# Attention rebuilt around pairs of heads, rows scattered into one region per expert, and slots read at a dynamic offset

## The chip, the core and the metric

One core of a Trainium2 chip. Five engines work side by side, each through its own instruction queue: PE (matmul; its weight loads are shown as PEld), DVE (vector), ACT (scalar), POOL and SP. SP issues most transfers; POOL issues those that cast or that scatter and gather by index. The metric is the device time of one launch in microseconds (us). The kernel before takes 1003.38 us (median of 3 runs, 1003.16 to 1006.25).

## The reference

Linear attention over 8 batch elements (B), 8 heads (H), 576 positions (S) and 64 dimensions (D), then a mixture of 8 experts of which each row uses one.

```python
def phi(x, c, s):                       # c, s: cosine and sine of the position
    r = np.maximum(x, 0.0)
    return np.concatenate([r * c, r * s], axis=-1)
q_p, k_p = phi(q, cos_w, sin_w), phi(k, cos_w, sin_w)
kv  = np.einsum('bhsf,bhsd->bhfd', k_p, v)
num = np.einsum('bhsf,bhfd->bhsd', q_p, kv)
den = np.einsum('bhsf,bhf->bhs', q_p, np.sum(k_p, axis=2))[..., None] + 1e-06
x   = (num / den)                       # to [B*S, H*D] = [4608, 512]
logits = x @ w_gate
e_idx  = np.argmax(logits, axis=1)
gate_w = softmax(logits)[np.arange(N), e_idx]
eom    = 1.0 / (1.0 + np.exp(-(x @ w_output_gate)))
for e in range(8):                      # w1: [512, 1024], w2: [1024, 512]
    mask = e_idx == e
    out[mask] = gate_w[mask, None] * eom[mask, e, None] * (np.maximum(x[mask] @ w1[e], 0) @ w2[e])
```

## The kernel before

**Start.** POOL issues the 16 loads of the expert weights (w1t, w2t, lines 121 and 122; f32 in memory, f16 on the core, so POOL's queue q0 casts them). SP's queue q1 takes everything else in.

**Attention**, for each batch element b. The 576 positions go in five chunks c of 128 (the last of 64), one position per partition. For each chunk SP loads qt, kt, vt for all heads (lines 147 to 151; a run of 64 numbers, 256 bytes, is one packet). ACT writes the cosine and sine halves of qp, DVE those of kp. PE multiplies kp by vt per head into kvp (line 171; the 65th column of vt is 1, which gives the sum of k_p), and DVE adds kvp to kvzg. PE transposes qp per head (tp, line 178), and ACT and DVE in turn copy that to qpt. Behind the five chunks PE transposes kvzg per head (tpk) and multiplies it by both gate matrices (kvgp), so that 16 columns of gate terms stand beside the 65. A second pass over the chunks multiplies qpt by the 81 columns per head (fx, line 204); DVE divides, sums the gate terms over the heads (glog), takes maximum, one-hot (oh_tab) and coefficient (coef_tab), and SP stores the row block xch as f16 to x_dram.

All f32 operations of PE are recorded twice per matmul, once per transpose.

**Routing** starts when all 40 chunks are done. Counts per chunk and expert give each expert's start among 42 slots of 128 rows. Then, chunk by chunk, PE ranks the rows, DVE forms dst_i, and POOL scatters the pair (row number, coefficient) to the table bucket (line 348). The table is read back (bidx) and gives the row indices for gather and scatter.

**Experts.** For each of 42 slots: PE reads the slot's expert into a register; POOL gathers 128 rows of x_dram into xg (line 371); PE transposes xg (xtsp), DVE copies that to xts; PE multiplies by w1t (hp, line 395), ACT rectifies into hs; in the next round of the loop PE transposes hs (htsp), DVE copies that to hts, PE multiplies by w2t (yp, line 406), DVE scales into ysb (line 410), and POOL scatters ysb to the output (line 411).

The order on each engine is made by a scheduler from the written program; an engine executes its rows in that order.

Of the kernel before, what the change touches and what calls it, by code (L numbers as in the profile page):

```python
# [10 lines left out]
F32 = mybir.dt.float32  # L12
F16 = mybir.dt.float16
I32 = mybir.dt.int32
ALU = mybir.AluOpType
# [5 lines left out]
def kernel(  # L21
# [24 lines left out]
    NCH = 5  # L46
    ROWS = [128, 128, 128, 128, 64]
    NG = B * NCH
    NSLOT = 42
    CAP = NSLOT * P  # L50
# [3 lines left out]
    tabs = ctx.enter_context(tc.tile_pool(name="tabs", bufs=1))  # L54
    dram = ctx.enter_context(tc.tile_pool(name="drampool", bufs=1, space=bass.MemoryType.DRAM))

    x_dram = dram.tile([N, DM], F16, name="x_dram")
    bucket = dram.tile([CAP, 2], F32, name="bucket")

# [3 lines left out]
    make_identity(nc, ident16[:])  # L63
    u128 = constp.tile([P, P], F32, name="u128")
    make_upper_triangular(nc, u128[:], val=1.0, diag=False)
    ones128 = constp.tile([P, P], F32, name="ones128")
    GP.memset(ones128[:], 1.0)

    s_i = constp.tile([P, NCH], I32, name="s_i")
    GP.iota(s_i[:], pattern=[[128, NCH]], base=0, channel_multiplier=1)  # L70
    th = constp.tile([P, NCH], F32, name="th")
# [3 lines left out]
    th2 = constp.tile([P, NCH], F32, name="th2")  # L75
# [5 lines left out]
    cosc = constp.tile([P, NCH], F32, name="cosc")  # L81
    sinc = constp.tile([P, NCH], F32, name="sinc")

    def поly(dst, coeffs, extra_mul, nm):
        acc = constp.tile([P, NCH], F32, name=nm)
        DVE.memset(acc[:], 0.0)
        for cc in reversed(coeffs):
            DVE.tensor_mul(acc[:], acc[:], th2[:])
            DVE.tensor_scalar_add(acc[:], acc[:], float(cc))
        DVE.tensor_mul(acc[:], acc[:], th2[:])  # L90
        DVE.tensor_scalar_add(acc[:], acc[:], 1.0)
        if extra_mul is not None:
            DVE.tensor_mul(dst[:], acc[:], extra_mul[:])
        else:
            DVE.tensor_copy(dst[:], acc[:])

    поly(sinc, sin_c, th, "acc_s")
    поly(cosc, cos_c, None, "acc_c")

    wg2 = constp.tile([P, H, 16], F32, name="wg2")  # L100
    SP.dma_start(wg2[0:64, :, 0:8], moe_w_gate.rearrange("(h p) e -> p h e", p=64))
    SP.dma_start(wg2[0:64, :, 8:16],
                 moe_w_output_gate.rearrange("(h p) e -> p h e", p=64))

    iota8 = constp.tile([P, E], F32, name="iota8")
    _i8 = constp.tile([P, E], I32, name="_i8")
    GP.iota(_i8[:], pattern=[[1, E]], base=0, channel_multiplier=0)
    DVE.tensor_copy(iota8[:], _i8[:])
    iota_slot = constp.tile([P, 1], F32, name="iota_slot")
    _is = constp.tile([P, 1], I32, name="_is")  # L110
    GP.iota(_is[:], pattern=[[1, 1]], base=0, channel_multiplier=128)
    DVE.tensor_copy(iota_slot[:], _is[:])
    mvals = constp.tile([P, NSLOT], F32, name="mvals")
    _im = constp.tile([P, NSLOT], I32, name="_im")
    GP.iota(_im[:], pattern=[[128, NSLOT]], base=0, channel_multiplier=0)
    DVE.tensor_copy(mvals[:], _im[:])
# [3 lines left out]
    for e in range(E):  # L120
# [3 lines left out]
    coef_tab = tabs.tile([P, NG], F32, name="coef_tab")  # L124
    oh_tab = tabs.tile([P, NG, E], F32, name="oh_tab")
    bidx = tabs.tile([P, NSLOT, 2], F32, name="bidx")
    gidx_i = tabs.tile([P, NSLOT], I32, name="gidx_i")
    sidx_i = tabs.tile([P, NSLOT], I32, name="sidx_i")
    slote_i = tabs.tile([P, 1], I32, name="slote_i")

    with tc.tile_pool(name="attn_b", bufs=2) as ap, \
         tc.tile_pool(name="attn_c", bufs=2) as ap2, \
         tc.tile_pool(name="pskv", bufs=3, space=bass.MemoryType.PSUM) as pskv, \
         tc.tile_pool(name="psgen", bufs=5, space=bass.MemoryType.PSUM) as psgen:

        for b in range(B):
            qpt = ap.tile([P, H, 576], F32, name=f"qpt{b}", tag="qpt")
            kvzg = ap.tile([P, H, 81], F32, name=f"kvzg{b}", tag="kvzg", bufs=1)
            GP.memset(kvzg[:], 0.0)

            for c in range(NCH):
                rows = ROWS[c]
                s0 = c * 128
                qt = ap2.tile([P, H, D], F32, name=f"qt{b}_{c}", tag="qt")
                kt = ap2.tile([P, H, D], F32, name=f"kt{b}_{c}", tag="kt")
                vt = ap2.tile([P, H, 65], F32, name=f"vt{b}_{c}", tag="vt")
                SP.dma_start(qt[0:rows, :, :],
                             q[b, :, s0:s0 + rows, :].rearrange("h s d -> s h d"))
                SP.dma_start(kt[0:rows, :, :],
                             k[b, :, s0:s0 + rows, :].rearrange("h s d -> s h d"))  # L150
                SP.dma_start(vt[0:rows, :, 0:64],
                             v[b, :, s0:s0 + rows, :].rearrange("h s d -> s h d"))
                GP.memset(vt[:, :, 64:65], 1.0)  # L153

                qp = ap2.tile([P, H, P], F32, name=f"qp{b}_{c}", tag="qp")
                kp = ap2.tile([P, H, P], F32, name=f"kp{b}_{c}", tag="kp")
                ACT.activation(qp[0:rows, :, 0:64], qt[0:rows, :, :], AF.Relu,
                               scale=cosc[0:rows, c:c + 1])
                ACT.activation(qp[0:rows, :, 64:128], qt[0:rows, :, :], AF.Relu,
                               scale=sinc[0:rows, c:c + 1])  # L160
                DVE.tensor_scalar(kp[0:rows, :, 0:64], kt[0:rows, :, :], 0.0,
                                  cosc[0:rows, c:c + 1], ALU.max, ALU.mult)
                DVE.tensor_scalar(kp[0:rows, :, 64:128], kt[0:rows, :, :], 0.0,
                                  sinc[0:rows, c:c + 1], ALU.max, ALU.mult)

                for hg in range(2):
                    kvp = pskv.tile([P, 4, 65], F32, name=f"kvp{b}_{c}_{hg}",
                                    tag="kvps")
                    for hh in range(4):
                        h = hg * 4 + hh  # L170
                        PE.matmul(kvp[:, hh, :], kp[0:rows, h, :],  # L171
                                  vt[0:rows, h, :], start=True, stop=True)
                    DVE.tensor_tensor(kvzg[:, hg * 4:(hg + 1) * 4, 0:65],  # L173
                                      kvzg[:, hg * 4:(hg + 1) * 4, 0:65], kvp[:],
                                      ALU.add)
                for h in range(H):
                    tp = psgen.tile([P, P], F32, name=f"tp{b}_{c}_{h}", tag="ps")
                    PE.transpose(tp[:, 0:rows], qp[0:rows, h, :],  # L178
                                 ident[0:rows, 0:rows])
                    if h % 2 == 0:  # L180
                        ACT.copy(qpt[:, h, s0:s0 + rows], tp[:, 0:rows])  # L181
                    else:
                        DVE.tensor_copy(qpt[:, h, s0:s0 + rows], tp[:, 0:rows])  # L183

            for h in range(H):
                tpk = psgen.tile([P, P], F32, name=f"tpk{b}_{h}", tag="ps")
                PE.transpose(tpk[0:64, :], kvzg[:, h, 0:64], ident[:, :])  # L187
                kvt_sb = tabs.tile([P, P], F32, name=f"kvt{b}_{h}", tag="kvt")
                ACT.copy(kvt_sb[0:64, :], tpk[0:64, :])  # L189
                kvgp = psgen.tile([P, 16], F32, name=f"kvgp{b}_{h}", tag="ps")  # L190
                PE.matmul(kvgp[:, :], kvt_sb[0:64, :], wg2[0:64, h, :],  # L191
                          start=True, stop=True)
                DVE.tensor_copy(kvzg[:, h, 65:81], kvgp[:, :])

            for c in range(NCH):
                rows = ROWS[c]
                s0 = c * 128
                g = b * NCH + c
                n0 = b * S + s0

                fx = [psgen.tile([P, 4, 81], F32, name=f"fx{g}_{i}", tag="ps")
                      for i in range(2)]
                for h in range(H):
                    PE.matmul(fx[h // 4][0:rows, h % 4, :],  # L204
                              qpt[:, h, s0:s0 + rows], kvzg[:, h, 0:81],
                              start=True, stop=True)
# [240 lines left out]
```

## Time and profile before

| | us |
|---|---|
| median of the runs | 1003.38 |
| profiled execution, span of the core | 1002.1 |
| first packets to first dense matmuls (kvp) | 0 to 121.6 |
| attention, one batch element | 62.26 |
| scatters to the table bucket | 610.8 to 792.9 |
| first hp matmul to the end of the last yp | 804.05 to 990.8 |

Share of the span that each engine is busy: PE 66%, DVE 38%, ACT 18%, POOL 15%. A row of the profile names line, engine, operation and the tiles (out<-in); PE's records overlap, so the time per matmul is read from start to start. Behind a row stands how long the engine was idle before it, and what ended that.

### The profile page before, as it was taken

What the parts mean: (1) busy time and instruction counts of PE and PEld (TensorE: products, weight loads), DVE (VectorE), ACT (ScalarE), POOL (GpSimd) and SP (SyncE); (2) the same over time, 40 slices, a digit from 0 to 9 for tenths busy, and PEclk for the clock granted to TensorE, in tenths of its full rate; (3) what the DMA queues carried; (4) which work ended last, traced back from release to release, by engine and by line L of the source; (5) the groups of instructions that cost most, each with busy time, mean ns of one, the idle gap of its engine ahead of it and who ended that gap; (6) DMA issues with size and microseconds to landing.
All of it is one profiled execution on the core that took longest, in us unless ns stands there. A gap on an engine that the chain in (4) does not pass through costs nothing.

```text
span 1002.1 us, 11193 instructions
## 1 busy us (share of the span) xinstructions
PE 662.7 (66%) x3257; PEld 496.6 (50%) x3257; DVE 377.0 (38%) x2049; ACT 177.9 (18%) x509; POOL 152.0 (15%) x245
## 2 busy tenths in 40 slices
PE   0113187997979979799797884223221099999994
PEld 0013176785867858578575683222211045555552
DVE  3101028456283562835528364111111033443342
ACT  1111001314123141231412210000000022222221
POOL 4110000000000000000000001222222134444441
PEclk9999999999999999999999999999999999999998
DMA  9999931412414124141241000000000112222220
GB/s 173 200 200 200 78 79 34 101 42 61 85 50 95 43 61 85 51 95 43 61 84 51 11 17 9 0 0 2 0 0 1 6 63 91 84 83 88 86 85 21
DMA packets 148858, 65.64 MB, mean 65 GB/s; under 512 B 128254, under 2 KB 141054, under 8 KB 148800
## 3 DMA queue, kind: packets, MB, share of 16 engines
q1 hardware_dynamic: 129600, 33.16, 17.5%
q0 software_dynamic: 19200, 31.77, 13.8%
q8 instruction: 29, 0.48, 0.2%
q14 instruction: 29, 0.24, 0.1%
HBM read 67.45 MB, written 15.81 MB: 83 GB/s over the span
## 4 chain that ended last, share of the span: by engine, by line
PE 50%; DMA 26%; DVE 13%; ACT 5%; issue 4%; SPq 1%; POOLq 0%; POOL 0%; ACTq 0%; DVEq 0%
DMA bucket<-pack,dst_i 14%; PE kvp L171 13%; PE fx L204 9%; PE hp L395 7%; DMA qt<-in_q_dram 7%; PE yp L406 7%; PE tp L178 5%; PE kvgp L191 4%; DVE xch L250 4%; DVE glog L215 2%; PE tpk L187 2%; DMA kt<-in_k_dram 2%; PE htsp L384 2%; DMA vt<-in_v_dram 2%; ACT kvt L189 1%
## 5 line engine op out<-in xcount | busy, mean ns | idle before, releaser
L178 PE MATMUL tp<-ident,qp 128*128 128x128 f32 (+1 forms) x320 | 101.2, 423 | 113.9 <-ACT qpt L181 36.9
L171 PE MATMUL kvp<-vt,kp 128*128 128x65 f32 (+1 forms) x640 | 145.6, 412 | 30.5 <-DMA vt<-in_v_dram 28.1
L171 PEld LDWEIGHTS kvp<-vt,kp 128*128 128x128 f32 (+1 forms) x640 | 143.3, 332 | 32.9 <-issue 32.0
L204 PE MATMUL fx<-kvzg,qpt 128*128 128x81 f32 (+1 forms) x640 | 136.1, 406 | 7.4 <-DVE glog L215 7.4
L204 PEld LDWEIGHTS fx<-kvzg,qpt 128*128 128x128 f32 (+1 forms) x640 | 128.9, 310 | 12.2 <-PE fx L204 10.6
L178 PEld LDWEIGHTS tp<-ident,qp 128*128 128x128 f32 (+1 forms) x320 | 55.4, 206 | 158.2 <-ACT qpt L181 74.1
L399 ACT ACTIVATE hs<-hp 128x512 f16<-128x512 f32 x84 | 50.2, 597 | 331.5 <-PE hp L395 331.5
L250 DVE TENSOR_SCALAR xch<-fx,rc 128x64 f16<-128x64 f32 (+1 forms) x320 | 86.8, 273 | 0.0
L395 PE MATMUL hp<-w1t,xts 128*128 x336 | 81.2, 385 | 7.5 <-DVE xts L390 7.5
L406 PE MATMUL yp<-w2t,hts 128*128 x336 | 79.4, 379 | 1.1 <-DVE hts L387 1.1
L173 DVE TENSOR_TENSOR kvzg<-kvzg,kvp 128x260 f32<-128x260 f32 x80 | 32.9, 418 | 110.5 <-PE kvp L171 110.5
L410 DVE TENSOR_SCALAR ysb<-yp,bidx 128x512 f32<-128x512 f32 x42 | 31.5, 751 | 112.8 <-PE yp L406 112.8
L215 DVE SCALAR_TENSOR_TENSOR glog<-fx,rc,glog 128x16 f32<-128x16 f32 (+1 forms) x280 | 62.9, 225 | 0.3
L181 ACT COPY qpt<-tp 128x128 f32<-128x128 f32 (+1 forms) x160 | 39.8, 252 | 119.5 <-PE tp L178 119.5
L183 DVE COPY qpt<-tp 128x128 f32<-128x128 f32 (+1 forms) x160 | 38.6, 266 | 47.8 <-PE tp L178 45.3
L341 DVE CAST dst_i<-dst_f 128x1 int32<-128x1 f32 (+1 forms) x40 | 6.1, 152 | 131.8 <-DMA bucket<-pack,dst_i 131.8
L406 PEld LDWEIGHTS <-hts 128*128 128x128 f16 x336 | 32.8, 98 | 40.6 <-DVE hts L387 1.2
L153 POOL MEMSET vt<- 128x8 f32 x40 | 4.4, 113 | 314.2 <-PE kvp L171 263.2
L395 PEld LDWEIGHTS <-xts 128*128 128x128 f16 x336 | 32.1, 98 | 39.7 <-DVE xts L390 9.1
L411 POOL DMA_INDIRECT out_dram<-ysb,sidx_i x42 | 42.6, 1014 | 56.1 <-DVE ysb L410 37.2
L348 POOL DMA_INDIRECT bucket<-pack,dst_i x40 | 38.6, 966 | 79.3 <-DVE dst_f L338 55.6
L371 POOL DMA_INDIRECT xg<-x_dram,gidx_i x42 | 40.8, 972 | 62.6 <-PE xtsp L377 45.9
(234 smaller groups left out, 661.1 us busy)
## 6 DMA issues: line engine op xcount, KB each, us to landing
qt<-in_q_dram SPq DMA_DIRECT2D x32, 256.0 KB, 3.9
w1t<-in_moe_w_dram POOLq DMA_DIRECT2D x8, 1024.0 KB, 46.4
kt<-in_k_dram SPq DMA_DIRECT2D x32, 256.0 KB, 3.5
vt<-in_v_dram SPq DMA_DIRECT2D x32, 256.0 KB, 3.2
w2t<-in_moe_w_dram POOLq DMA_DIRECT2D x8, 1024.0 KB, 44.0
x_dram<-xch SPq DMA_DIRECT2D x32, 128.0 KB, 1.7
qt<-in_q_dram SPq DMA_DIRECT2D x8, 128.0 KB, 2.8
kt<-in_k_dram SPq DMA_DIRECT2D x8, 128.0 KB, 3.4
```

What stands on the lines that cost most here:

```text
L171: PE.matmul(kvp[:, hh, :], kp[0:rows, h, :], vt[0:rows, h, :], start=True, stop=True)
L178: PE.transpose(tp[:, 0:rows], qp[0:rows, h, :], ident[0:rows, 0:rows])
L181: ACT.copy(qpt[:, h, s0:s0 + rows], tp[:, 0:rows])
L191: PE.matmul(kvgp[:, :], kvt_sb[0:64, :], wg2[0:64, h, :], start=True, stop=True)
L204: PE.matmul(fx[h // 4][0:rows, h % 4, :], qpt[:, h, s0:s0 + rows], kvzg[:, h, 0:81], start=True, stop=True)
L215: DVE.scalar_tensor_tensor(glog[0:rows, :], fx[h // 4][0:rows, h % 4, 65:81], rc[0:rows, h:h + 1], glog[0:rows, :], ALU.mult, ALU.add)
L250: DVE.tensor_scalar(xch[0:rows, h * 64:(h + 1) * 64], fx[h // 4][0:rows, h % 4, 0:64], rc[0:rows, h:h + 1], None, ALU.mult)
L371: GP.indirect_dma_start(out=xg[:], out_offset=None, in_=x_dram[:, :], in_offset=bass.IndirectOffsetOnAxis(ap=gidx_i[:, j:j + 1], axis=0))
L395: PE.matmul(hp[:], xts[:, kc, :], w1t[:, kc, bass.ds(ev, 1), fh * 512:(fh + 1) * 512], start=(kc == 0), stop=(kc == 3))
L399: ACT.activation(hs[:, fh * 512:(fh + 1) * 512], hp[:], AF.Relu)
L406: PE.matmul(yp[:], hts[:, fc, :], w2t[:, fc, bass.ds(evp, 1), :], start=(fc == 0), stop=(fc == 7))
L411: GP.indirect_dma_start(out=out[:, :], out_offset=bass.IndirectOffsetOnAxis(ap=sidx_i[:, jj:jj + 1], axis=0), in_=ysb[:], in_offset=None, ...
```

## The change

**Layout.** Batch elements are taken in pairs (4 pairs). The first 512 positions of an element are laid four to a partition, so that one packet of q, k or v is 1024 bytes; the loads are for four heads at once (half hf). The last 64 positions of both elements of a pair share one tile of 128 partitions (the tails, still in packets of 256 bytes).

**Cosine and sine move from k to v, and from q to the result.** k is rectified once by ACT. DVE scales v by cosine and sine into the two halves of a block of 130 columns per head (tiles vcs, with cosine and sine themselves as columns 65 and 130). One matmul per head and chunk then has 64 columns loaded and 130 streamed, and two heads write the lower and upper 64 partitions of the same bank. q is transposed for two heads at a time without cosine and sine; the product of a head uses 64 rows of the array and 162 streamed columns, and ACT (t) and DVE (u) put the two halves together with cosine and sine.

```diff
+                    for pr in range(2):
+                        for ab in range(2):
+                            h = pr + 2 * ab
+                            lhs = (kt[:, h, c, :] if c < 4
+                                   else ktl[p0:p1, 4 * hf + h, :])
+                            PE.matmul(kvp[64 * ab:64 * ab + 64, hf,
+                                          130 * pr:130 * pr + 130],
+                                      lhs, w[p0:p1, h, :],
+                                      start=(c == 0 and pr == 0), stop=(c == 4),
+                                      skip_group_check=True)
...
+            for qd in range(4):
+                PE.transpose(tp[:, qd, :], qrf[:, 128 * qd:128 * qd + 128], ident[:])
...
+            ACT.activation(qT[:], tp[:], AF.Relu)
...
+                            PE.matmul(qo[:, 2 * ab + pr, 0:162], qT[r0:r0 + 64, qd, :],
+                                      kvms[b][r0:r0 + 64, 2 * qd:2 * qd + 2, :],
+                                      start=True, stop=True)
...
+                ACT.activation(t[:], qo[:, :, 0:81], AF.Copy, scale=cosc[:, c:c + 1])
+                DVE.scalar_tensor_tensor(u[:, 4 * hf:4 * hf + 4, :], qo[:, :, 81:162],
+                                         sinc[:, c:c + 1], t[:], ALU.mult, ALU.add)
...
+            GP.tensor_tensor(xrow[:, 0:DM].bitcast(F16).rearrange("p (h d) -> p h d", d=D),
+                             u[:, :, 0:64],
+                             rc[:].unsqueeze(2).to_broadcast([P, H, D]), ALU.mult)
```

The gate terms are made by four transposes and four matmuls per element instead of eight of each. PE's rows before, in batch 1's pass over k and q (tp transposes one head, kvp is the product of k and v for four heads, one after another):

```order
L171 MATMUL kvp_2_0_1444<-vt_2_1433,kp_2_1439 128x65 x4
L171 MATMUL kvp_2_1_1450<-vt_2_1433,kp_2_1439 128x65 x4
L178 MATMUL tp_3_1_1508<-ident,qp_3_1487 128x128
L178 MATMUL tp_3_2_1511<-ident,qp_3_1487 128x128
L178 MATMUL tp_3_3_1514<-ident,qp_3_1487 128x128
```

PE's rows now, in a pass over q (qtp transposes two heads, qo is the product for four heads):

```order
L311 MATMUL qo_0_0_1040<-kvm_931,qT_0_1037 128x162 x4
L311 MATMUL qo_0_1_1048<-kvm_931,qT_0_1037 128x162 x4
L300 MATMUL qtp_2_1102<-ident,qr_2_1099 128x128 x3
L311 MATMUL qo_1_0_1075<-kvm_931,qT_1_1072 128x162 x4
L311 MATMUL qo_1_1_1083<-kvm_931,qT_1_1072 128x162 x4
L300 MATMUL qtp_2_1102<-ident,qr_2_1099 128x128
```

The transposes of a chunk are half as many, and a matmul's output has twice the columns.

**Routing per pair.** x_dram and bucket are gone. Each expert has a region of 4608 rows in xs, and base holds how far each is filled. After the nine chunks of a pair, DVE and ACT make one-hot, coefficient and position for all of them at once (route), PE ranks with ten short f16 matmuls, and POOL writes row number and coefficient behind each row (meta) and scatters the whole row, 516 numbers of 16 bits, to its place:

```diff
+            DVE.tensor_tensor(base[:], base[:], rk[:, GC, :], ALU.add)
+            for c in range(GC):
+                xr = xrows[c]
+                GP.tensor_copy(xr[:, DM:DM + 4].bitcast(F32), meta[:, c, :])
+                GP.indirect_dma_start(
+                    out=xs[:, :],
+                    out_offset=bass.IndirectOffsetOnAxis(ap=di[:, c:c + 1], axis=0),
+                    in_=xr[:], in_offset=None)
```

At the start SP fills the first 128 rows of each region with zeros (nine stores). POOL's rows before, in the bucket phase (ni numbers the rows of a chunk; DMASW is a scatter's landing):

```order
L348 DMA bucket<-pack_5020,dst_i_5018 5376x2 [waits DMASW7_49,DMASW6_49,DVE_49]
L344 IOTA ni_5081 64x1 [waits DVE_49]
L348 DMA bucket<-pack_5068,dst_i_5066 5376x2 [waits DMASW7_49,DVE_49]
L344 IOTA ni_5093 128x1 [waits DVE_49]
L348 DMA bucket<-pack_5080,dst_i_5078 5376x2 [waits DMASW0_49,DVE_49]
```

POOL's rows now, behind the second routing step (xr is a row block, the xrow of the code):

```order
L391 DMA xs<-xr_0_1028,di_1501 36992x516 [waits DMASW0_49,DVE_49,Pool_49]
L391 DMA xs<-xr_1_1063,di_1501 36992x516 [waits DMASW1_49,Pool_49]
L391 DMA xs<-xr_2_1098,di_1501 36992x516 [waits DMASW2_49,Pool_49]
L333 TENSOR_TENSOR xr_0_1619<-u_0_1630,rc_0_1647 128x512 [waits DVE_49]
L391 DMA xs<-xr_3_1133,di_1501 36992x516 [waits DMASW3_49,Pool_49]
L333 TENSOR_TENSOR xr_1_1654<-u_1_1665,rc_1_1682 128x512 [waits DVE_49]
```

The scatters moved from behind attention into it; each waits for the one before, as it did. Of the weight loads, the last six stand on POOL between the first xrow steps. Behind the last pair DVE works out, for each of 43 slots, the expert (evs), the first row (rows_i) and which rows are the slot's own (valid).

**Slots.** SP fetches a slot's 128 rows two slots ahead, as one block at an address from a register; a predicated copy takes the valid row numbers into sidx, by which the output is scattered. PE's and SP's order in this stage is the written one.

```diff
+        def fetch(j):
+            rj = SP.value_load(rows_i[0:1, j:j + 1], min_val=0, max_val=E * REG)
+            xg = fsb.tile([P, XW], U16, name=f"xg{j}", tag="xg", bufs=5)
+            SP.dma_start(xg[:], xs[bass.ds(rj, 128), :])
...
+                DVE.copy_predicated(sidx[:, j:j + 1], valid[:, j:j + 1],
+                                    xg[:, DM:DM + 2].bitcast(I32))
...
-                DVE.tensor_scalar(ysb[:], yp[:], bidx[:, jj, 1:2], None, ALU.mult)
+                DVE.tensor_scalar(ysb[:], yp[:], xgp[:, DM + 2:DM + 4].bitcast(F32),
+                                  None, ALU.mult)
```

DVE's rows before, one repeating pair of slots:

```order
L410 TENSOR_SCALAR ysb_5916<-yp_5907,bidx 128x512
L390 COPY xts_5948<-xtsp_5932 128x512
L387 COPY hts_5946<-htsp_5937 128x1024
L390 COPY xts_6004<-xtsp_5988 128x512
L410 TENSOR_SCALAR ysb_5972<-yp_5963,bidx 128x512
L387 COPY hts_6002<-htsp_5993 128x1024
```

DVE's rows now, in which every slot is like the next:

```order
L517 COPY xts_3043<-xtsp_3026 128x512
L514 COPY hts_3041<-htsp_3032 128x1024
L504 COPY_PREDICATED sidx<-valid,xg_3081 128x1
L537 TENSOR_SCALAR ysb_3067<-yp_3058,xg_2817 128x512
L517 COPY xts_3109<-xtsp_3092 128x512
```

Of two slots before, one has its xts ahead of the other's ysb; now each xts stands behind a ysb.

More of the change, by code (lines that the diff above doesn't have):

```diff
@@ L108 @@
[L108 to L116, printed above, removed]
+    poly(sinc, sin_c, th, "acc_s")
@@ new lines @@
+    DVE.tensor_copy(pv[:], pv_i[:])
+    low = constp.tile([P, E, E], F32, name="low")
+    DVE.tensor_tensor(low[:], iota8[:].unsqueeze(2).to_broadcast([P, E, E]),
+                      iota8[:].unsqueeze(1).to_broadcast([P, E, E]), ALU.is_ge)
+    base = constp.tile([P, E], F32, name="base")
+    DVE.tensor_copy(base[:], reg0[:])
+    oh16s = []
+    for i in range(2):
+        t = constp.tile([P, GC + 1, E], F16, name=f"oh16_{i}")
+        GP.memset(t[:, GC, :], 0.0)
+        oh16s.append(t)
@@ L366 @@
         st = {}
         for j in range(NSLOT + 1):
+            if j + 2 < NSLOT:
+                fetch(j + 2)
             if j < NSLOT:
[L369 to L374 removed]
+                ev = PE.value_load(evs[0:1, j:j + 1], min_val=0, max_val=7)
+                xg = ahead.pop(j)
```

601 lines of the change are left out of this document (332 added, 269 removed).

## The prediction

> **What bounds the kernel now.** I read the stages first, then the chain of work that ended last, then the rows inside each stage. Busy time in four stretches (length, then busy us and count of PE, PEld, DVE, ACT, POOL, then clock, DMA share, GB/s):
>
> ```profile
> 0.00:100.00 100.00, 16.95 (x72) 14.09 (x72) 17.41 (x74) 13.66 (x33) 16.72 (x40) 1.00 1.13 193
> ...
> 269.40:331.66 62.26, 53.78 (x225) 44.67 (x225) 32.94 (x198) 15.85 (x54) 1.20 (x6) 1.00 0.30 67
> ...
> 610.00:793.00 183.00, 47.98 (x187) 36.04 (x187) 29.57 (x266) 0.00 (x0) 43.35 (x78) 1.00 0.01 1
> ...
> 804.00:980.00 176.00, 168.48 (x1116) 90.55 (x1114) 66.31 (x119) 47.77 (x80) 77.00 (x79) 1.00 0.25 83
> ```
>
> Four regimes: 100 us of full DMA engines and idle PE; attention, one batch element every 62.26 us with PE busy 53.78; 183 us in which no engine is busy for more than 26%; and the expert stage, PE full. The start, by DMA queue between 20 and 100 us (packets, MB, share of 16 engines), and by the chain:
>
> ```profile
> q0 software_dynamic: 9984, 13.52, 93.8%
> q1 hardware_dynamic: 9864, 2.48, 23.6%
> ...
> 103.44 18.05 DMA vt<-in_v_dram
> ```
>
> The weight queue q0 and the queue q1 of q, k and v send packet for packet, 9984 to 9864. A pair takes 80 us x 16 / 9924 = 129 ns, and a q1 packet is only 252 B, so batch 0 is complete at 121.5 us. The third regime, by the chain:
>
> ```profile
> 610.83 3.60 DMA bucket<-pack,dst_i
> 615.47 3.82 DMA bucket<-pack,dst_i
> ```
>
> Each of 40 scatters waits for the one before: one per 4.64 us, 3.6 of them landing.
>
> **Attention.** Eight transposes a chunk became four (tp, now qtp); each matmul of the q pass (fx, now qo) uses half the array and streams 162 columns instead of 81, each of the key pass (kvp) 130 instead of 65. Prices, from PE in order of time and from the groups by shape:
>
> ```profile
> 178.34 2.16 PE L178 MATMUL tp<-ident,qp 128*128 128x128 f32 x7 [0.30 <-ACT qpt L181]
> ...
> 394.78 7.88 PE L204 MATMUL fx<-kvzg,qpt 128*128 128x81 f32 x36
> ...
> 411.94 1.31 PE L204 MATMUL fx<-kvzg,qpt 128*64 128x81 f32 x8 [0.68 <-DVE glog L215]
> ...
> L204 PE MATMUL fx<-kvzg,qpt 128*128 128x81 f32 x512 | 115.5, 420 | 2.5 <-DVE glog L215 2.5
> ...
> L204 PE MATMUL fx<-kvzg,qpt 128*64 128x81 f32 x128 | 21.2, 347 | 4.9 <-DVE glog L215 4.9
> ```
>
> An f32 matmul leaves two records. Start to start they take (7.88 - 0.42) / 35 = 0.213 us where 128 columns are loaded, and (1.31 - 0.35) / 7 = 0.137 where 64 are. Both fit 1.67 ns times the larger of columns loaded and columns streamed (128 gives 0.213, 81 gives 0.135). By this a record that streams 130 takes 0.217, one that streams 162 takes 0.270, if two halves of the array never work together; half of that if they do. No row of before shows two halves side by side. Between these ends I take the value nearest to a row: the 0.213 period is a 128-column load, and loads queue one behind another there, so I let the streams of two halves overlap and the loads not. A transpose takes (2.16 - 0.44) / 6 = 0.28.
>
> Per batch: key-value products 80 records x 0.108 = 8.7. Gate step 4 x 0.28 + 8 x 0.213 = 2.8. A q chunk 4 x 0.28 + 16 x 0.213 = 4.5, four of them 18.1. The tail chunk of a pair of batches (32 records of 64 loaded columns in four quarters, 0.135 each, and its transposes) 5.4, or 2.7 per batch. Sum 32.3 us of PE, against 53.78. Waits on top: 62.26 / 53.78 = 1.157 as before. Ends: full overlap (a q record 0.135) gives 27.3, none gives 46.8.
>
> The other engines stay below that. Rows:
>
> ```profile
> L161 DVE TENSOR_SCALAR kp<-kt,cosc 128x512 f32<-128x512 f32 x32 | 15.4, 480 | 23.3 <-DMA kt<-in_k_dram 23.2
> ...
> L173 DVE TENSOR_TENSOR kvzg<-kvzg,kvp 128x260 f32<-128x260 f32 x80 | 32.9, 418 | 110.5 <-PE kvp L171 110.5
> ...
> L220 DVE TENSOR_REDUCE lmax<-glog 128x1 f32<-128x8 f32 x32 | 4.8, 150 | 0.0
> ...
> L157 ACT ACTIVATE qp<-qt,cosc 128x512 f32<-128x512 f32 x32 | 23.1, 722 | 64.4 <-DMA qt<-in_q_dram 54.6 <-DVE cosc L95 5.7 <-PE tp L178 4.0
> ...
> L250 DVE TENSOR_SCALAR xch<-fx,rc 128x64 f16<-128x64 f32 x256 | 69.9, 275 | 0.0
> ...
> L348 POOL DMA_INDIRECT bucket<-pack,dst_i x40 | 38.6, 966 | 79.3 <-DVE dst_f L338 55.6 <-DVE rank L327 16.6 <-DVE pack L347 3.2
> ...
> L139 POOL MEMSET kvzg<- 128x648 f32 x8 | 5.1, 640 | 147.5 <-DVE xch L250 147.5
> ```
>
> DVE per batch: 28 scalings and copies of 256 elements at some 0.33 (between 0.275 and 0.48), nine additions out of PSUM at 0.48, some 35 small steps at 0.15 to 0.25: about 20 us. ACT: two rectifications of 1024 elements at 1.25 (0.72 for 512, and as much again less a start), 4.5 chunks x 1.5: about 11.
>
> POOL gets work that before doesn't show, the normalised rows xrow (128x512): bounded below by the memset (0.64) and above by the same result on DVE in eight pieces (8 x 0.275 = 2.2); I take 1.4. In the Trainium skill the page "GPSIMD Engine Reference", section "3. Performance versus the Vector engine", puts a two-input GpSimd operation at about 2.6 cycles per element; my estimate from it is 1.1 us, and no run here shows it.
>
> By the order of POOL's rows a scatter still waits for the landing of the last one, but now 27 of 36 stand under attention, between the xrow steps. Queued behind such a wait are the xrow steps, and u (two buffers) waits for them. Price of one, between the rows
>
> ```profile
> bucket<-pack,dst_i POOLq DMA_INDIRECT x40, 3.6
> ...
> out_dram<-ysb,sidx_i POOLq DMA_INDIRECT x42, 2.8
> ```
>
> and the 4.64 above: I take 3.7. A pair then needs 9 x (3.7 + 1.4) + 1.4 = 47 us of POOL, 24 per batch: hidden under 37. With 2.2 for xrow and 4.64 it would be 31, still hidden; only where halves overlap in full would POOL and not PE set the pace.
>
> **The start.** SP issues a transfer in some 0.6 us:
>
> ```profile
> 1.52 0.61 SPq L102 DMA_DIRECT2D wg<-n_moe_w_output_gate_dram  x1
> ```
>
> First come four gate loads and nine region fillers (1152 packets of 1 KB, of which I let 450 go before the weights are in flight at 7 us), then batch 0 (six halves of 512 packets and 2048 packets of the pair's tails) and k and v of batch 1 (2048), which PE takes ahead of batch 0's q. Packets of q, k and v outside the tails are now 1024 B. A pair costs between 129 ns and 129 + 33 (768 B more at the 23 B/ns that 27 MB read for 13.52 written and 2.48 MB make per engine); I take 146. So q of batch 0 begins at 7 + (702 + 5120 + 2048) x 0.146 / 16 = 79, say 80 us (70 to 87). The last six of 16 weight loads stand on POOL behind xrow steps; they end near 115, long before their use.
>
> From 80 us: 8 x (18.1 + 2.7) + 6 x 8.7 + 7 x 2.8 = 238 of PE, x 1.157 = 276: attention ends at **356**; before, the scatters behind it begin at 610.83.
>
> **Between the stages.** Routing of the last pair cannot hide: some 26 small steps on DVE and ACT, ten short matmuls and nine copies, 12 us; nine scatters x 3.7 = 33; fetch and first transposes 4. Sum 49 (41 to 58), in place of 183 and more. The slot arithmetic (about 25 DVE steps) lies under the scatters.
>
> **The expert stage.** In DVE's order of before every second copy xts, which PE's hp group needs, stood ahead of ysb, which empties yp; now each stands behind one. What that costs, in order of time:
>
> ```profile
> 899.40 0.39 PE L377 MATMUL xtsp<-ident,xg 128*128 128x128 f16 x4
> ...
> 899.60 0.75 DVE L410 TENSOR_SCALAR ysb<-yp,bidx 128x512 f32<-128x512 f32 x1 [2.55 <-PE yp L406]
> ...
> 900.27 0.41 DVE L390 COPY xts<-xtsp 128x512 f16<-128x512 f16 x1
> ...
> 900.83 1.89 PE L395 MATMUL hp<-w1t,xts 128*128 x8 [0.37 <-DVE xts L390]
> ...
> 902.56 1.89 PE L406 MATMUL yp<-w2t,hts 128*128 x8
> 904.28 0.61 PE L384 MATMUL htsp<-ident,hs 128*128 128x128 f16 x8
> 904.73 1.89 PE L395 MATMUL hp<-w1t,xts 128*128 x8
> ...
> 908.18 0.39 PE L377 MATMUL xtsp<-ident,xg 128*128 128x128 f16 x4
> ```
>
> The slot with xts behind ysb takes 904.28 - 899.40 = 4.88, the other 3.90; the mean is 4.39. I expect 4.88 in all 43 slots: 210 us instead of 42 x 4.39 = 184. If PE is not held up so, 189.
>
> The remaining ends:
>
> ```profile
> 804.05 3.60 PE L395 MATMUL hp<-w1t,xts 128*128 x8
> ...
> 988.91 1.89 PE L406 MATMUL yp<-w2t,hts 128*128 x8 [1.09 <-DVE hts L387]
> ...
> span 1002.1 us, 11193 instructions
> ```
>
> 990.8 - 804.05 is 2.4 more than 42 x 4.39, and 11.3 follow. **Sum:** 356 + 49 + 210 + 2.4 + 11.3 = 629 of span, +1.3 as before between span and median (1003.38 against 1002.1): **630 us**.
>
> **Rivals.**
> - Full overlap of halves, loads too: 27.3 per batch, 8 x 15.8 + 52 + 20 = 198, x 1.157 = 229, end of attention 309, total 583. For it: operands lie on disjoint halves. Against: loads set the period in L204. The Trainium skill states it as a rule ("TensorEngine Tiling (Array Packing)", section "Key Properties": tiles load and multiply in parallel); no run here shows it yet.
> - The change doesn't do what it says, halves run one after another: 8 x 26.7 + 6 x 17.3 + 20 = 338, x 1.157 = 391, end 471, total 745. For it: PE's rows before are strictly in line.
> - Changing between whole and split array empties PE. The order has 110 such places in attention; at 0.42 - 0.213 = 0.2 us, the part of a matmul that normally overlaps the next, 22 us more, and with chunk chains (transpose, ACT, matmul, ACT, DVE) exposed in as many places perhaps as much again: 675. The same section of the skill says that a change of mode drains the engine.
> - Slower than before: scattering whole 1 KB rows is not like scattering 8 B. With L from issue to landing, POOL sets attention, 80 + 4 x (9 (L + 1.5) + 1.4), then 16 + 9 L and 225 behind it. That passes 1003 from L = 13.8 us on. Against: 2 KB rows landed in 2.8.
>
> **How the numbers follow.** Forecast 0.45, full overlap 0.22, no overlap 0.2, drains and chains 0.11, slow scatters 0.02. The range takes in most of the first and third case, widened by the start (9 us either way), the slots (21 less) and the scatters (9): 560 to 748. Within 0.3%, which is about what a measurement of this kernel tells from no change, I see 0.01; slower 0.02; faster 0.97.
>
> **What would show it.** Steps: q of batch 0 on PE near 80 us; batches every 37; records of kvp 0.108 apart, of qo 0.213; 36 scatters 3.7 apart; last qo to first hp 49; slots of 4.88 with PE waiting for xts. The prediction is wrong if split matmuls follow each other at 0.27, if u waits for POOL in every chunk, or if a fetch lands later than 3.9 us after ysb frees its buffer, since the predicated copy on DVE then holds back the next ysb.

## The result, and the profile after

The changed kernel takes 575.73 us (median of 4 runs, 572.66 to 581.29) where the kernel before, on the same chip, takes 1004.52 us: a ratio of 0.572, with a 95% interval of 0.570 to 0.574. Forecast were 630 us, with a range of 560 to 748. Medians here and below are over all runs of a kernel; where runs that lie more than 1.5% above the fastest of their kernel (slow runs) bear on a comparison, the single times stand beside the median.

The head of the page of the changed kernel, to hold against the start of the prediction (PEclk is the clock granted to PE in 40 slices of the span, in tenths):

```profile
span 570.9 us, 8672 instructions
...
PE 352.1 (62%) x2764; PEld 231.0 (40%) x2764; DVE 255.9 (45%) x851; ACT 138.1 (24%) x239; POOL 140.6 (25%) x189
...
PEclk9985659776597959789966555999999999999998
DMA  7999988999083708450310012112222222222200
```

The stages (from, to and length; busy us and count of PE, PEld, DVE, ACT, POOL; clock, DMA share, GB/s). The cuts are the first q-pass matmul, 200 us, the end of the last q-pass matmul, the first hp and the last hp:

```profile
0.00:81.50 81.50, 15.10 (x114) 12.39 (x114) 21.41 (x144) 7.51 (x9) 11.02 (x32) 0.76 1.07 215
81.50:200.00 118.50, 71.53 (x686) 56.89 (x684) 65.59 (x228) 37.51 (x67) 31.26 (x38) 0.79 0.77 187
200.00:310.60 110.60, 77.77 (x752) 60.98 (x753) 76.12 (x259) 40.68 (x75) 45.13 (x58) 0.82 0.33 95
310.60:350.50 39.90, 1.17 (x15) 0.92 (x16) 11.62 (x51) 1.00 (x3) 11.05 (x19) 0.50 0.11 37
350.50:557.50 207.00, 182.49 (x1177) 97.92 (x1177) 79.06 (x167) 50.76 (x85) 40.17 (x41) 0.99 0.22 73
```

The last yp ends at 562.7. So the span is 81.5 + 229.1 + 39.9 + 212.2 + 8.2, against the forecast 80 + 276 + 49 + 212.4 + 11.3. Nearly all of the difference is in attention, and there PE is busy for only 71.5 + 77.8 = 149 of 229 us: 18.7 per batch, where 32.3 were forecast.

PE in order of time (start, length, matmul records; a later group starts before the modelled end of the one ahead):

```profile
31.90 3.48 PE L252 MATMUL kvp<-vcs,k 128*64 128x130 f32 x32 [31.90 <-DVE vcs L245]
...
85.34 2.40 PE L252 MATMUL kvp<-vcs,k 128*64 128x130 f32 x32
...
91.55 1.38 PE L311 MATMUL qo<-kvm,qT 64*128 64x162 f32 x16 [1.12 <-ACT qT L302]
92.85 0.33 PE L300 MATMUL qtp<-ident,qr 128*128 128x128 f32 x1
...
120.94 2.53 PE L311 MATMUL qo<-kvm,qT 64*128 64x162 f32 x16 [4.21 <-ACT qT L302]
...
264.93 2.00 PE L252 MATMUL kvp<-vcs,k 128*64 128x130 f32 x32 [2.04 <-ACT kvc L266]
```

The pass over q by its group (busy, mean ns of one record, idle time ahead of it):

```profile
L311 PE MATMUL qo<-kvm,qT 64*128 64x162 f32 x512 | 56.0, 359 | 41.9 <-DVE u L323 32.1 <-ACT qT L302 9.8
```

With 0.36 us for the last record, q records stand (1.38 - 0.36) / 15 = 0.068 us apart at 91.55 and (2.53 - 0.36) / 15 = 0.145 at 120.94. Key records stand (2.00 - 0.27) / 31 = 0.056 apart at 264.93, where the clock is full throughout. In the group at 31.90 they stand 0.108 apart up to 34.8; the first change of the clock on record in this trace, to full, comes at 35.0. The group at 85.34 has such a change inside it, at 86.2, so that its mean of (2.40 - 0.36) / 31 = 0.066 belongs to neither speed; the 0.066 in the first expectation below is this mixed value.

One form has two speeds, about a factor of two apart, where the PEclk row moves between 5 and 9 tenths. The kernel before has the two speeds too: eight f16 hp matmuls took 3.60 us at 804.05 and 1.89 at 900.83 (both rows stand in the prediction). Its clock column says 1.00 at both, for the first change of clock that this trace records comes only at 807.5 us (818 on the trace's own clock, which one expectation below quotes); there the hp matmuls go from 0.43 us apart to 0.22. Ahead of it 1.00 is what stands where nothing is on record. All f32 prices in the prediction came from that stretch.

### The profile page after: what moved, and what is told of

It is laid out like the page before. It is cut to its first block, busy times and chain, and to the rows that moved or that the text cites. A ratio compares the mean times of both kernels' runs of the same rounds, so it can differ in the third digit from the quotient of the medians.

```text
span 570.9 us, 8672 instructions
## 1 busy us (share of the span) xinstructions
PE 352.1 (62%) x2764; PEld 231.0 (40%) x2764; DVE 255.9 (45%) x851; ACT 138.1 (24%) x239; POOL 140.6 (25%) x189
## 5 line engine op out<-in xcount | busy, mean ns | idle before, releaser
L252 PE MATMUL kvp<-vcs,k 128*64 128x130 f32 x512 | 48.7, 347 | 63.6 <-DVE vcs L245 57.5
L539 POOL DMA_INDIRECT out_dram<-ysb,sidx x43 | 42.1, 980 | 177.2 <-DVE ysb L537 163.7
L311 PE MATMUL qo<-kvm,qT 64*128 64x162 f32 x512 | 56.0, 359 | 41.9 <-DVE u L323 32.1
L333 POOL TENSOR_TENSOR xr<-u,rc 128x512 f16<-128x512 f32 x36 | 39.6, 1104 | 128.0 <-DVE rc L327 127.5
L537 DVE TENSOR_SCALAR ysb<-yp,xg 128x512 f32<-128x512 f32 x43 | 32.3, 751 | 82.8 <-PE yp L533 82.8
L252 PEld LDWEIGHTS kvp<-vcs,k 128*64 128x64 f32 x512 | 39.6, 177 | 71.0 <-issue 57.1
L323 DVE SCALAR_TENSOR_TENSOR u<-qo,sinc,t 128x324 f32<-128x324 f32 x72 | 38.9, 551 | 64.0 <-ACT t L322 36.4
L311 PEld LDWEIGHTS qo<-kvm,qT 64*128 64x128 f32 x512 | 45.1, 221 | 51.2 <-DVE u L323 36.4
L391 POOL DMA_INDIRECT xs<-xr,di x36 | 37.7, 1047 | 89.9 <-DMA xs<-xr,di 63.3
L322 ACT ACTIVATE t<-qo,cosc 128x324 f32<-128x324 f32 x72 | 37.7, 529 | 57.0 <-PE qo L311 42.2
```

Of the source, the lines that this page charges most:

```text
L252: PE.matmul(kvp[64 * ab:64 * ab + 64, hf, 130 * pr:130 * pr + 130], lhs, w[p0:p1, h, :], start=(c == 0 and pr == 0), stop=(c == 4), skip_g ...
L311: PE.matmul(qo[:, 2 * ab + pr, 0:162], qT[r0:r0 + 64, qd, :], kvms[b][r0:r0 + 64, 2 * qd:2 * qd + 2, :], start=True, stop=True)
L322: ACT.activation(t[:], qo[:, :, 0:81], AF.Copy, scale=cosc[:, c:c + 1])
L323: DVE.scalar_tensor_tensor(u[:, 4 * hf:4 * hf + 4, :], qo[:, :, 81:162], sinc[:, c:c + 1], t[:], ALU.mult, ALU.add)
L333: GP.tensor_tensor(xrow[:, 0:DM].bitcast(F16).rearrange("p (h d) -> p h d", d=D), u[:, :, 0:64], rc[:].unsqueeze(2).to_broadcast([P, H, D] ...
L391: GP.indirect_dma_start(out=xs[:, :], out_offset=bass.IndirectOffsetOnAxis(ap=di[:, c:c + 1], axis=0), in_=xr[:], in_offset=None)
```

## The experiments

**Halves in line.** Does the order of the matmuls make the halves overlap?

```diff
-                for pr in range(2):
-                    qd = 2 * hf + pr
-                    for ab in range(2):
-                        r0 = 64 * ab
+                for ab in range(2):
+                    r0 = 64 * ab
+                    for pr in range(2):
+                        qd = 2 * hf + pr
```

(the same in stage_k)

> Both passes emit two matmuls of one half of the array and then two of the other, instead of alternating; nothing else is changed. Theory A (the two halves work at the same time, and the clock follows how much of the array streams): at most one matmul in two now finds the other half free, so at the full clock a q record goes from 0.068 us apart to about 0.10 (0.137 / 2 times 3 / 2), a key record from 0.066 to about 0.10, and the mean granted clock in attention (0.60 to 0.93 in the changed kernel's stretches from 60 to 310 us) falls. Theory B (halves do not overlap; matmuls run at twice the speed for another reason): spacing and clock stay as they are. For the time: if PE set the pace of attention, some 5 us more per batch at the full clock and 10 at half, 40 to 80 us in all; if it does not, under 15.

Measured: 576.79 us, ratio 0.575 (0.572 to 0.578): no difference that can be told. PE:

```profile
93.05 1.48 PE L311 MATMUL qo<-kvm,qT 64*128 64x162 f32 x16 [1.12 <-ACT qT L302]
```

(1.48 - 0.36) / 15 = 0.075 us per record instead of 0.068, not the 0.10 expected, though two matmuls of one half now follow each other. In the trace their starts still come in pairs, 14 ns apart at first and some 30 later, where they had been 7. Records of one half alone stand 0.137 us apart (the run on one half, below), so a pair is most likely one matmul of each half: those of the second half start beside those of the first, past two that were written ahead of them. The trace doesn't name the half of a record, so this is inferred. The edit did not take the overlap away, and this run decides nothing about its price; the run on one half, below, does.

**The q pass twice.** Does PE set the pace of attention?

```diff
-                        if c < 4:
+                        for rpt in range(2 if c < 4 else 0):
                             PE.matmul(qo[:, 2 * ab + pr, 0:162], qT[r0:r0 + 64, qd, :],
```

> Each q-pass matmul of the four full chunks of a batch is issued twice with the same operands and the same destination: 512 records more. If PE sets the pace of attention, as the prediction had it, they cost 512 x 0.0685 = 35 us at the full clock and 70 at half, and the span grows by about that. If loads and the chain of ACT, DVE and POOL set it, the span grows by less than 15 us, and the granted clock in attention rises above the 0.60 to 0.93 of the changed kernel, because the array works more of the time.

Measured: 593.33 us, 17.6 more than the changed kernel. From the groups by shape: 

```profile
L311 PE MATMUL qo<-kvm,qT 64*128 64x162 f32 x1024 | 99.4, 348 | 40.1 <-DVE u L323 20.3 <-ACT qT L302 19.5
```

Its 512 additional records cost 99.4 - 56.0 = 43 us of PE and 17.6 of time; both expectations (35 or more, under 15) missed. The mean clock between the first and the last q matmul rose to 0.86, from 0.79 and 0.82. PE holds the pace for part of attention, beside something else for the rest.

**Weights paced.** A one-element copy from the first normalised chunk of batch b into the weight tiles holds back the loads of expert b:

```diff
+    def load_w(e, xr):
+        one = xr[0:1, 0:1].bitcast(F16)
+        GP.tensor_copy(w1t[0:1, 0, e, 0:1], one)
+        GP.tensor_copy(w2t[0:1, 0, e, 0:1], one)
```

> The two weight loads of an expert wait for the first normalised chunk of the batch of the same number (a one-element copy into the weight tile stands ahead of each), so that none is in flight before batch 0's q pass; in the changed kernel ten of 16 were issued by 23 us. If the weights share the DMA engines packet for packet with q, k and v at the start, the first q-pass matmul moves from 81.5 us to between 40 and 50, and the whole kernel becomes 25 to 45 us shorter. If the total of bytes before the expert stage is the limit, the start is earlier but the end of attention (310) moves by less than 10. If something else holds the start, the first q-pass matmul stays at 80.

Measured: 532.35 us, 43.4 less. The stages up to the first hp, cut at the first q-pass matmul, 150 us and the end of the last q-pass matmul:

```profile
0.00:33.80 33.80, 13.43 (x114) 10.76 (x114) 20.12 (x146) 7.40 (x9) 2.49 (x22) 0.91 0.80 209
33.80:150.00 116.20, 77.94 (x738) 61.19 (x736) 69.10 (x239) 39.88 (x71) 37.77 (x51) 0.76 0.83 198
150.00:271.10 121.10, 76.93 (x700) 60.35 (x701) 68.31 (x247) 38.71 (x71) 48.73 (x70) 0.75 0.78 166
271.10:311.90 40.80, 1.16 (x14) 0.92 (x15) 11.53 (x52) 1.00 (x3) 11.13 (x19) 0.50 0.11 36
```

The q pass starts at 33.8 instead of 81.5, 47.7 earlier, sooner than the 40 to 50 expected; attention ends 39.5 earlier and takes 237 us instead of 229, since the weights now load beside it (DMA share 0.78 in its second half, where it was 0.33). So the weights held the start, as the prediction read it. That the two queues share the engines packet for packet is borne out roughly: between 20 and 80 us of the changed kernel q0 sent 6383 packets and q1 7235.

**Next slot's xts ahead of this slot's ysb.** turn(j) holds the lines that made xtsp, sidx and xts of slot j, and is called a slot earlier, ahead of yp:

```diff
+            if j + 1 < NSLOT:
+                xt_next = turn(j + 1)
             if j >= 1:
...
                 yp = ps_y.tile([P, DM], F32, name=f"yp{jj}", tag="yp")
```

> In the expert stage the transposes and the copy xts of the next slot are written ahead of the yp matmuls and ysb of this slot; all else is the same. If the copy standing behind ysb on DVE is what holds PE, as the prediction had it, slots fall from 4.88 us to between 3.9 and 4.4, and the kernel is 42 x 0.5 to 42 x 0.98 = 21 to 41 us shorter. If PE is short of something else in a slot (order of its own groups, the landing of the fetch), slots stay above 4.7 and the time within 8 us.

Measured: 545.19 us, 30.5 less. First a slot of the changed kernel, then one of this run:

```profile
443.36 1.89 PE L522 MATMUL hp<-w1t,xts 128*128 x8 [0.60 <-DVE xts L517]
...
447.02 0.75 DVE L537 TENSOR_SCALAR ysb<-yp,xg 128x512 f32<-128x512 f32 x1 [1.80 <-PE yp L533]
...
447.68 0.41 DVE L517 COPY xts<-xtsp 128x512 f16<-128x512 f16 x1
...
448.25 0.59 PE L522 MATMUL hp<-w1t,xts 128*128 x2 [0.60 <-DVE xts L517]
```

```profile
441.79 1.89 PE L529 MATMUL hp<-w1t,xts 128*128 x8
...
443.94 0.43 DVE L504 COPY xts<-xtsp 128x512 f16<-128x512 f16 x1 [1.05 <-PE xtsp L499]
...
445.46 0.61 PE L520 MATMUL htsp<-ident,hs 128*128 128x128 f16 x8
445.67 0.75 DVE L546 TENSOR_SCALAR ysb<-yp,xg 128x512 f32<-128x512 f32 x1 [1.03 <-PE yp L542]
445.91 0.81 PE L529 MATMUL hp<-w1t,xts 128*128 x3
```

A slot goes from 448.25 - 443.36 = 4.89 us to 445.91 - 441.79 = 4.12 (mean over all slots, start to start, 4.88 and 4.13). PE no longer waits: xts is made while yp runs.

**Rows on DVE** instead of POOL:

```diff
-            GP.tensor_tensor(xrow[:, 0:DM].bitcast(F16).rearrange("p (h d) -> p h d", d=D),
+            DVE.tensor_tensor(xrow[:, 0:DM].bitcast(F16).rearrange("p (h d) -> p h d", d=D),
```

> The normalised rows xr (128x512, 1.10 us on POOL) are made on DVE, so that no step that u waits for stands behind a scatter on POOL. It adds 36 steps of some 0.6 us to DVE (between 0.55 for 324 elements of u and 1.1), 22 us, 2.7 per batch. If POOL's rows behind scatters hold attention (u waited 27.5 us for them in the changed kernel, up to 5.2 at once), attention ends 10 to 25 us earlier. If loads set the pace up to 165 us and DVE after it, the time is the same or up to 15 us longer.

Measured: 538.64 us, 37.1 less, more than the 10 to 25 expected. In the changed kernel, by the waits between the first and the last q-pass matmul (total us, times, longest):

```profile
POOL xs L391 <- DMA xs<-xr,di: 44.0, 16, 6.1
...
PE qo L311 <- DVE u L323: 32.1, 18, 5.6
DVE u L323 <- POOL xr L333: 27.5, 11, 5.2
```

With the rows on DVE the third wait is gone and the second is 20.2. Up to batch 2, whose first row is made at 161.2 us instead of 171.5, the run gains 10 us in a way that I had not seen: POOL, with no rows to wait for, issues the last weight load at 64.8 us instead of 123.0. From there on the gain is some 25 us, about the wait removed. That it came from the place in the queue, and not from the shorter step, is argued from these waits; no run separated the two. The price of a row, 128x512:

```profile
L333 POOL TENSOR_TENSOR xr<-u,rc 128x512 f16<-128x512 f32 x36 | 39.6, 1104 | 128.0 <-DVE rc L327 127.5
```

1.10 us on POOL in the changed kernel, 0.685 on DVE here.

**Routing by batch** instead of by pair (glog, the one-hot and the index tiles per batch):

```diff
-            if b % 2 == 1:
-                route(g, glog, xrows)
+            route(b, glog, xrows)
```

> Routing and scatters are done after every batch instead of after every pair, so that five scatters instead of nine stand behind the last q pass. Price of a scatter in that chain 3.4 us (317.43 to 344.44 in the changed kernel, eight periods): 4 x 3.4 = 13.5 us less, if the four additional routings (26 small DVE steps, 5 us each) find room beside attention. If they don't, between 0 and 10 us less or some longer. The stretch from the last q matmul to the first hp falls from 40 to 26 in either case.

Measured: 569.03 us, 6.7 less. The stretch from the last q matmul to the first hp fell from 39.9 to 26.0 as expected; attention ended at 322.7 instead of 310.6 and took most of it back. POOL's rows stood behind more scatters: the wait of u for them went from 27.5 to 36.9 us.

**The four together.**

> Weights paced, xts first, rows on DVE, routing by batch, together. If their gains add up: 575.7 - 43.4 - 30.5 - 13.5 and 0 to 25 for the rows = 463 to 488 us. If earlier loads and earlier ends only bring the same DMA limit nearer (45 MB of q, k, v and weights at the 220 to 240 GB/s of full slices are 190 to 205 us, plus 225 behind attention), it stops near 490 to 510.

Measured: 476.78 us, ratio 0.475 (0.471 to 0.479). Its four runs lie wide apart: 471.44, 473.36, 480.19 and 486.56. Single gains add up to 118 us, measured are 99 on the median and 103 on the two lower runs. Attention, and POOL behind it:

```profile
34.00:249.20 215.20, 155.17 (x1446) 123.22 (x1445) 158.12 (x599) 80.33 (x150) 53.54 (x93) 0.79 0.83 192
```

```profile
255.64 1.04 POOL L396 DMA_INDIRECT xs<-xr,di  x1 [0.23 <-POOL xr L395]
264.69 1.02 POOL L396 DMA_INDIRECT xs<-xr,di  x1 [8.02 <-DMA xs<-xr,di]
268.30 0.97 POOL L396 DMA_INDIRECT xs<-xr,di  x1 [2.59 <-DMA xs<-xr,di]
```

The DMA engines are busy for 0.83 of attention, no engine for more than 0.74, and one scatter waits 8.0 us: the last weight load was issued at 250.64 and took 12.8 us to land.

**The kernel before with 128 columns** streamed per f32 matmul. The extra columns are neighbouring data:

```diff
                     PE.matmul(fx[h // 4][0:rows, h % 4, :],
-                              qpt[:, h, s0:s0 + rows], kvzg[:, h, 0:81],
+                              qpt[:, h, s0:s0 + rows], kvw[:, h * 81:h * 81 + P],
                               start=True, stop=True)
```

(and kvp likewise; kvw is kvzg with a flat index)

> The kernel before, with both its f32 passes streaming 128 columns instead of 65 (kvp) and 81 (fx); the extra columns are neighbouring data that nothing reads. Weight loads of 128 columns set the 0.213 us from record to record there, and the changed kernel has 0.213 for 128 f32 columns where the granted clock is 0.5 and 0.109 where it is 1.0. So attention of the kernel before ran at half clock, although the column says 1.00 there (the first change of the clock is on record at 818 us). Theory A (the clock follows how much the array streams, and two halves at work raise it): with 128 columns the array streams nearly all of the time that records take, the clock rises, and 1004 us become 800 to 950, with more work. Theory B (f32 matmuls or their pauses keep the clock down, and the columns don't matter): 995 to 1015 us, records still 0.213.

Measured: 933.60 us, ratio 0.930 (0.928 to 0.932): more work, and 71 us less. Two stretches of attention (the clock is on record from 81 us on in this run), and PE:

```profile
100.00:269.00 169.00, 124.19 (x657) 105.00 (x657) 94.30 (x568) 36.25 (x131) 5.53 (x35) 0.68 0.43 77
269.00:331.00 62.00, 49.99 (x248) 40.08 (x249) 38.36 (x220) 21.24 (x71) 1.83 (x11) 0.67 0.34 80
```

```profile
358.20 2.03 PE L209 MATMUL fx<-kvzg,qpt 128*128 128x128 f32 x16
```

At 358 us, with the clock at 1.0, 16 records take 2.03 us: less the last one (0.3 to 0.4), 0.11 us from record to record, where the kernel before had 0.213; at half clock this run's records, too, stand 0.213 apart. In the kernel before, PE was busy for 53.78 of 62.26 us per batch and the clock stayed at half: a busy share of 86% was not enough. Here it is busy for 73 to 81% in the two stretches, and the clock is full for about a third of the time. The columns streamed per record are what was changed; the share of time in which PE is busy does not account for the clock.

**All on one half.**

```diff
-                        r0 = 64 * ab
+                        r0 = 0
```

> All matmuls of the q pass read rows 0 to 63 (the upper half's heads are replaced by the lower half's, so the output is not the reference's); number, shapes and order of the matmuls are those of the changed kernel, only no two can lie on different halves. If the halves overlap in the changed kernel, a q record takes 0.137 us at the full clock and 0.27 at half instead of 0.072 and 0.137, PE gets 512 x 0.065 = 33 us more at the full clock and up to 68 at half, and the granted clock in attention does not rise. Time: by the run with the q matmuls doubled (17.6 us longer for 512 more records, 38 us more of PE) some 17 to 35 us longer than 575.7, since loads and POOL hold attention beside PE. If they don't overlap (matmuls only run faster), spacing and time stay within 3 us.

Measured: 606.47 us, 30.7 more than the changed kernel. One chunk in PE's order of time, then the pass by its group, then attention from the first q matmul to the last:

```profile
96.90 2.47 PE L311 MATMUL qo<-kvm,qT 64*128 64x162 f32 x16
```

```profile
L311 PE MATMUL qo<-kvm,qT 64*128 64x162 f32 x512 | 114.9, 394 | 17.8 <-DVE u L323 10.5 <-ACT qT L302 7.3
```

```profile
82.00:341.00 259.00, 222.40 (x1438) 190.13 (x1436) 142.92 (x487) 78.89 (x142) 75.43 (x95) 0.68 0.49 126
```

(2.47 - 0.39) / 15 = 0.139 us per record against 0.068, both at the full clock; the pass takes 114.9 us of PE against 56.0, and the clock in attention falls to 0.68. That is the price of the overlap in the q pass, with what it does to the clock: 31 us of time. The key pass was not taken apart in this way.

**Three together**, without the routing by batch, and **four with weights and fillers moved**:

> Weights paced, xts first and rows on DVE, without the routing by batch. Against the run of four together (476.8) this prices the routing by batch there: alone it was worth 6.7 us. If DMA engines hold attention there, four more scatters behind attention (13.5 us) stand against 20 us of DVE saved under it: 480 to 492. If the routing by batch is what kept the four from adding up (458 by the single runs), 455 to 470.

> The four together, with the last expert's weights loaded in batch 6 instead of 7 (expert 6 late in batch 5), and the nine region fillers issued behind batch 0's loads instead of ahead of them. In the run of four together a scatter after the last q pass landed 8 us after its issue beside the last weight load (255.64 to 264.69 against 3.4 us for the others): 5 to 6 us less there; the fillers are 1.2 MB, 5 us at 235 GB/s, ahead of the first k: 4 to 5 us less. Together 463 to 470 us. If DMA bytes before 210 us hold attention, the earlier weights cost as much as they save, and it stays at 472 to 480.

Measured: 485.44 us (ratio 0.483, 0.481 to 0.484) and 473.31 us (0.469, 0.464 to 0.473). So in the combination the routing by batch is worth 8.7 us on the medians, and 13 against the two lower runs of the four together: no less than alone, and not what keeps the gains from adding up. Moving the weights and the fillers brought the first q matmul from 34.0 to 26.6 us and the last landing of 8 us went, but attention ended later, at 252.8 instead of 249.2. The runs of this kernel are 467.19, 472.46, 474.17 and one of 567.66 at a granted clock of 0.63; the first three lie about where the two lower runs of the four together do, so no gain can be told: the median lies at the lower edge of the second range that was expected (472 to 480), one run lies in the first.

What holds these two kernels is most likely the loads: 41 and 45 MB move during attention, at a DMA share of 0.83 and 0.86. No run took bytes away, so this is not shown.

## Why the prediction was right, and where it was not

The time lay within the range, near its lower end: 54 us below the forecast, and 7 below the 583 of the rival of full overlap. The mechanism was right in its outline: halves overlap, three quarters of the scatters move under attention, the slots lengthen. Inside attention two terms were wrong in opposite directions, and that the sum still came out in the range is in part luck. Term by term:

- **Start: right.** q of batch 0 at 81.5 us for 80 forecast. That the weights set it was shown by pacing them (33.8).
- **PE in attention: the step that failed.** I gave a q record 0.213 us and a key record 0.108, by letting the streams of two halves overlap and their weight loads not. Measured are 0.068 and 0.056 at the full clock and about 0.14 and 0.108 at half; so the key record was right for half clock, and the q record for neither. Two things were wrong. The loads do overlap: at the full clock records of 128 loaded columns in the whole array stand 0.11 us apart, and q records, with as many, 0.068; on one half the same pass takes twice as long. The rule of the Trainium skill that I set against my choice ("TensorEngine Tiling (Array Packing)", "Key Properties": tiles load and multiply in parallel) agrees with that: 0.068 against 0.139. And 1.67 ns per column was the price at half clock. I read the 1.00 of the clock column as measured, though the prediction itself quoted eight hp matmuls at 3.60 and at 1.89 us. The Trainium skill says that half clock is the default and that activity releases it ("TensorE: Matmul & The Clock Gate", "What's actually happening"); this trace agrees on the two states, but a PE that was busy for 86% of the time stayed at half in attention, and rose above it there only in the run that streamed 128 columns per record.
- **Waits on top of PE: failed the other way.** The factor of 1.157 from before became 229 / 149 = 1.53. The two errors cancel in part: attention took 229 us, 276 forecast. That 229 is also what the rival of full overlap gave is a coincidence: it had PE at 27.3 us per batch and the old factor. What replaced PE: loads until the weights are in (43 us less when paced) and rows behind scatters on POOL (some 25). The prediction dismissed POOL because its total (47 us a pair; xrow at 1.4 us, measured 1.10, which is also the estimate that the prediction drew from the Trainium skill's page "GPSIMD Engine Reference", section "3. Performance versus the Vector engine") was hidden. Its place in the queue was not: u waited up to 5.2 us at once for a row that stood behind a landing. I named this among what would make the prediction wrong, and gave it no price.
- **Between the stages: 9 too long.** 39.9 us for 49: routing 7 to the first scatter (12 forecast), and scatters 3.4 apart (3.7):

```profile
317.43 1.00 POOL L391 DMA_INDIRECT xs<-xr,di  x1 [0.27 <-POOL xr L390]
...
344.44 0.97 POOL L391 DMA_INDIRECT xs<-xr,di  x1 [2.43 <-DMA xs<-xr,di]
347.22 4.91 SPq L488 DMA_DIRECT2D xg<-xs  x5
...
350.48 1.86 PE L522 MATMUL hp<-w1t,xts 128*128 x4 [0.61 <-DVE xts L517]
```

- **Expert stage: right.** 4.88 us per slot on the mean and 212.2 in all, 212.4 forecast, and for the reason given: with xts moved ahead, slots fell to 4.13 on the mean.
- **The rivals.** No overlap is out: q records stand 0.068 us apart and 0.139 on one half, and the time rises there by 31 us. Full overlap is the one that came true on PE: loads overlap too. A price for changing between whole and split array does show, and it is small: the transposes at 92.85 start 0.225 us after the start of the last q record ahead of them (0.40 at half clock), where transposes follow one another in about 0.11 (0.21). 110 places at 0.12 to 0.19 us are an estimated 13 to 21 us of PE, close to the 22 of the prediction; at what the doubled q matmuls cost (17.6 us of time for 43 of PE) that would be 5 to 9 us of time. No run took it apart. Slow scatters are out: they stand 3.4 us apart, issue and landing together.

What stays open: how the 47 us of attention split between overlap and clock, since each raises the other (the clock fell to 0.68 when the overlap went), and the share of the key pass; and what holds the two fastest kernels.

## What to carry to other kernels

Before prices are taken from a stretch of a profile, find one form that occurs at both clocks, and see which of them the stretch shows; the clock column of these traces told nothing ahead of its first recorded change. An engine with time to spare can still set the pace by the order of its queue: a short step that others wait for should not stand behind a step that waits for a landing. And loads that are needed late belong behind those that are needed first, even where their queue is another one.

## What the runs showed of the hardware

- The clock of PE followed what the array streams, not the share of time in which PE is busy: with records 0.213 us apart and PE busy for 86% of the time, 65 and 81 columns streamed per 128 loaded left it at half, 128 columns brought it to 0.68 on the mean and saved 71 us.
- The two row halves of the array ran f32 matmuls side by side, starts 7 ns apart, and loads with them (0.068 us per record, 0.139 on one half); written two by two for one half, their starts still came in pairs, 14 ns apart.
- An f16 row block of 128x512 out of two f32 inputs took 1.10 us on POOL and 0.685 on DVE.
